# Attention steps inside the weight products: scores, transposes and output products put together behind twelve products

## The chip, the cores and the metric

One Trainium2 chip, one of its cores. The metric is the time of one execution on the device in microseconds (us); lower is better. TensorE is PE in the rows (its weight loads PEld), VectorE is DVE, ScalarE is ACT, GpSimd is POOL and SyncE, which issues most transfers, is SP.

## What is computed

Attention with two batches, 8 heads, 768 positions and a head size of 64; a query sees the first `n_global` positions and its own last `n_local`, with a bias by distance. Its output goes through two feed-forward layers.

```python
scores = scale * np.matmul(q, k.transpose(0, 1, 3, 2)) + bias
scores = np.where(keep, scores, -1000000000.0)
a = np.exp(scores - np.max(scores, axis=-1, keepdims=True))
a = a / (np.sum(a, axis=-1, keepdims=True) + 1e-09)
x = np.matmul(a, v)              # then 1536 tokens x 512
h = x @ w_in                     # 512 x 2048
x = (h * (1.0 / (1.0 + np.exp(-1.702 * h)))) @ w_out
h = np.maximum(x @ w2_in, 0.0)
out = h * h @ w2_out
```

## The kernel before

Attention is cut into 48 units: unit u is a tile of 128 queries and a pair of heads, so four units in a row make one tile of the attention's output. A unit has 256 keys, or 128 in the first tile of each batch. A unit passes through these helpers:

- `u_scores` (L243): two products on PE, one for each head, into two PSUM banks.
- `u_max` (L257): for each head one DVE operation that reads the scores from PSUM, adds the bias and takes the maximum, and a short read of the accumulator.
- `u_exp` (L280): on ACT.
- `u_norm`: on DVE a small addition (L271), a reciprocal (L273) and one multiply for each head (L318).
- `u_transpose` (L291, four on PE), `u_et` (L301, ACT copies them out of PSUM), `u_av` (L329, output products on PE).
- After the fourth unit of a tile: `x_hi` (L336, ACT) and `x_lo` (L341, DVE) split the output tile into two parts.

The first 19 units run in a stage of their own. The units from 19 on are woven into the first 16 steps of the feed-forward products. Step t has two half steps, each a call of `half(u, t, kind, block)`: the one of kind 0 holds the twelve products of `m_g1(t)` (L600) and that of kind 1 the twelve of `m_g2(t-1)` (L646); in step 0 the twelve of `m_g1(0)` are shared between both. In each half step the next weight slice is also prepared: `w_pre` (L464, ACT), `w_decode` in three DVE operations (L101, L105, L109), and `w_split`, whose upper part is copied by ACT (L486) and whose lower part is made on POOL (L487). In kind 0 the activation (`m_act`, L608, ACT) and `m_gate` (L626, DVE) follow the products; in kind 1 `m_split` splits the gated values on ACT (L616) and POOL (L617).

The schedule is manual: each engine runs its instructions in the order in which the code writes them, so that an instruction that waits holds up all behind it on its engine. Scores go to banks 5 and 6 (columns 0 to 255 of each), transposes to all of bank 5, outputs to bank 7. Bank 4 holds the products of `m_g1`. After the attention ends, at about 200 us of the span, the rest is feed-forward products that the change doesn't touch.

Of the kernel before, what the change touches and what calls it, by code (L numbers as in the profile page):

```python
# [8 lines left out]
F32 = mybir.dt.float32  # L9
# [105 lines left out]
def tile_kernel(ctx: ExitStack, tc: tile.TileContext, a: dict, out: bass.AP):  # L115
    nc = tc.nc
    ctx.enter_context(tc.manual_schedule())
    att = ctx.enter_context(tc.tile_pool(name="att", bufs=2))
    psum = ctx.enter_context(tc.tile_pool(name="psum", bufs=1, space=PSUM))
    banks = [psum.tile([128, 512], F32, name=f"bank{n}") for n in range(8)]  # L120
    turn = {}

    def ring(name, n, shape, dt=F32):
# [2 lines left out]
    def nxt(key, tiles):  # L126
        turn[key] = turn.get(key, -1) + 1
        return tiles[turn[key] % len(tiles)]
# [75 lines left out]
    nu = len(units)  # L204
    ur_t, uh_t, ul_t, sc_t, e_t, st_t, tr_t, et_t, xt_t = ({} for _ in range(9))

    start = [True]
# [13 lines left out]
    def bank(what):  # L221

        if start[0]:
            return nxt(what, {"av": banks[0:2], "sc": [banks[2:4], banks[4:6]], "tr": banks[6:8]}[what])

        return {"sc": banks[5:7], "tr": banks[5], "av": banks[7]}[what]

    def u_load(u):
        if u >= nu or u in ur_t:
# [6 lines left out]
    def u_scores(u):  # L236

        n = u_keys(u)[0]
        t = ur_t[u][0]
        ps = sc_t[u] = bank("sc")  # L240
        for e in range(2):
            h = slice(e * 64, e * 64 + 64)
            nc.tensor.matmul(  # L243
                ps[e][:, 0:n], lhsT=t[h, 0:128], rhs=t[h, 384 - n:384], start=True, stop=True
            )

    def u_keys(u):

        return (256, 0) if units[u][0] % QT else (128, 256)

    def u_max(u):
        p = units[u][1]
        ps = sc_t.pop(u)
        e_, st = e_r[u % 4], st_r[u % 4]
        n, d0 = u_keys(u)
        for e in range(2):
            nc.vector.tensor_tensor_reduce(  # L257
                out=e_[:, e, 0:n], in0=ps[e][:, 0:n], in1=dh[:, 2 * p + e, d0:d0 + n],
                scale=-0.125, scalar=3.0e38, op0=ALU.add, op1=ALU.min, accum_out=st[:, e:e + 1],
            )  # L260
        e_t[u], st_t[u] = e_, st
# [3 lines left out]
    def u_sum(u):  # L265

        if not 0 <= u < nu or sums.get(u) == 2:
            return
        st = st_t[u]
        if u not in sums:  # L270
            nc.vector.tensor_scalar_add(st[:, 4:6], st[:, 4:6], 1e-9)  # L271
        else:
            nc.vector.reciprocal(st[:, 6:8], st[:, 4:6])  # L273
        sums[u] = sums.get(u, 0) + 1

    def u_exp(u):
        e_, st = e_t[u], st_t[u]
        n = u_keys(u)[0]
        for e in range(2):
            nc.scalar.activation(  # L280
                out=e_[:, e, 0:n], in_=e_[:, e, 0:n], func=AF.Exp, scale=-1.0,
                bias=st[:, e:e + 1], accum_out=st[:, 4 + e:5 + e],
            )

    def u_transpose(u):
        e_ = e_t.pop(u)
        nb = u_keys(u)[0] // 128
        ps = bank("tr").rearrange("p (b q) -> p b q", b=2)
        for b in range(nb):
            for e in range(2):  # L290
                nc.tensor.transpose(  # L291
                    ps[:, b, e * 128:e * 128 + 128], e_[:, e, b * 128:b * 128 + 128], ident
                )
        tr_t[u] = ps

    def u_et(u, eng):
        ps = tr_t.pop(u)
        nb = u_keys(u)[0] // 128
        t = et_r[u % 2]
        if eng is nc.scalar:  # L300
            eng.copy(t[:, 0:nb], ps[:, 0:nb])  # L301
        else:
            eng.tensor_copy(t[:, 0:nb], ps[:, 0:nb])
        et_t[u] = t

    def u_norm(u, eng):
        u_sum(u)
        u_sum(u)
        e_, st = e_t[u], st_t.pop(u)
        n = u_keys(u)[0]  # L310
        if eng is nc.gpsimd:
            eng.tensor_tensor(
                out=e_[:, :, 0:n], in0=e_[:, :, 0:n],
                in1=st[:, 6:8].unsqueeze(2).to_broadcast([128, 2, n]), op=ALU.mult,
            )
        else:
            for e in range(2):
                eng.tensor_scalar_mul(e_[:, e, 0:n], e_[:, e, 0:n], st[:, 6 + e:7 + e])  # L318
# [19 lines left out]
    def x_lo(qt):  # L338
        c, i = divmod(qt, CH // 128)
        s = slice(i * 128, i * 128 + 128)  # L340
        nc.vector.tensor_tensor(  # L341
            out=xl[c][:, :, s], in0=xt_t.pop(qt), in1=xh[c][:, :, s].bitcast(F32), op=ALU.subtract
        )
# [29 lines left out]
    def u_out(u):  # L373
        if not 0 <= u < nu:
            return
        u_av(u)
        if units[u][1] == NP - 1:
            x_hi(units[u][0])
            los.append(units[u][0])

    def rest(inner):
# [41 lines left out]
        def plain(t):  # L423
            return steps[t][1] == 0
# [34 lines left out]
        def w_pre(kind, t):  # L459
            if (kind, t) not in raws or raws[kind, t][0] is None:  # L460
                return
            r, _ = raws[kind, t]
            c = mo.tile([128, 512], F32, tag=f"c{kind}", name=f"c{kind}", bufs=CB[kind])
            nc.scalar.activation(out=c, in_=r[:, :, 1].bitcast(F32), func=AF.Copy, scale=2.0 ** -112)  # L464
            raws[kind, t] = (r, c)

        def w_decode(kind, t, parts=range(3)):
            if (kind, t) not in raws or raws[kind, t][0] is None:
                return
            r, c = raws[kind, t]  # L470
            decode(nc, r, c, c, parts)
            ph, _, f = steps[t]
            if 2 in parts and kind == 1:
                nc.sync.dma_start(out=store[ph * NF + f], in_=c)
# [6 lines left out]
        def w_split(kind, t):  # L481
            if (kind, t) not in raws:
                return
            hi, lo = w_slot(kind, t)
            c = raws.pop((kind, t))[1]
            nc.scalar.copy(hi, c)  # L486
            nc.gpsimd.tensor_tensor(out=lo, in0=c, in1=hi.bitcast(F32), op=ALU.subtract)  # L487
            if kind == 1 or any(plan[t2][1] and uses[t2] == uses[t] for t2 in range(t + 1, T)):
                parts_out.append((kind, t, hi, lo))
# [99 lines left out]
        def h_bank(t):  # L589

            return banks[{0: 3, T0: 5, T0 + 1: 6}.get(t, 4)]
# [13 lines left out]
        def m_act(t):  # L605
            func, scale = ((AF.Tanh, 0.851), (AF.Relu, 1.0))[steps[t][0]]
            s = s_r[t % 2] if t >= T0 else sg[:, t % 3]
            nc.scalar.activation(out=s, in_=h_bank(t), func=func, scale=scale)  # L608
            g_t[t] = s

        def halves(x, n):

            return x[:, 1:3] if n else x[:, 0:8:7]
# [5 lines left out]
        def m_gate(t):  # L619
            s, h = g_t[t], h_bank(t)  # L620
            g = s
            if not plain(t):
                g = halves(g_p, t % 2)
                s, h = (x.rearrange("p (n k) -> p n k", n=2) for x in (s, h))
            if steps[t][0] == 0:
                nc.vector.scalar_tensor_tensor(out=g, in0=s, scalar=1.0, in1=h, op0=ALU.add, op1=ALU.mult)  # L626
            else:
                nc.vector.tensor_tensor(out=g, in0=h, in1=s, op=ALU.mult)  # L628


        def m_split(t):
            g = g_t[t]
            if t >= T0 and t % 2 == 0:
                ghl[t // 2 % 2] = mo.tile([128, 4, 512], F32R, tag="m4", name="ghl", bufs=2)
            gh, gl = (ghl[t // 2 % 2][:, t % 2 * 2 + n] for n in range(2))
            split(g, gh, gl, nc.vector if t >= T0 else nc.gpsimd)
            g_t[t] = (gh, gl)
# [273 lines left out]
        def half(u, t, kind, block):  # L911

            tw = t + 2 - kind
            w_pre(kind, tw)
            w_split(kind, tw - 1)
            block(0)
            if u < nu:
                u_scores(u)
            w_decode(kind, tw, (0,))
            w_decode(kind, tw, (1,))  # L920
            if u < nu:
                u_max(u)
                u_exp(u)
            block(1)
            if u <= nu:
                u_norm(u - 1, nc.vector)
            w_decode(kind, tw, (2,))
            if kind == (t == 0):
                m_act(t)
                m_gate(t)  # L930
            if kind == 1:
                m_split(t)
            if u - 2 < nu:
                u_transpose(u - 2)
                u_et(u - 2, nc.scalar)
            u_out(u - 3)
            if los:
                x_lo(los.pop())
            u_load(u + 4)

        u = n0 + 3
# [26 lines left out]
        for t in range(T0, T + LAG):  # L968
            q, e = divmod(t, 2)
# [306 lines left out]
```

## Time and profile before

| what | value |
|---|---|
| median of 3 runs (lowest, highest) | 647.03 us (645.46, 647.56) |
| the profiled execution's own time | 645.78 us |
| its span in the trace | 643.9 us |
| granted clock of TensorE, mean | 0.986 |
| PE busy | 617.9 us, 96% of the span |
| DVE busy | 480.6 us, 75% |
| ACT busy | 323.3 us, 50% |
| POOL busy | 93.1 us, 14% |

The span is what the trace covers; 1.9 us lie around it. Shares of busy time are means over stages that differ: the half steps lie between about 46 and 200 us.

### The profile page before, as it was taken

The numbers are of one execution on the slowest core, as the hardware profiler recorded it, in microseconds if no ns is written. First come the engines' busy times: TensorE is split into PE (matmuls) and PEld (weight loads), VectorE is DVE, ScalarE is ACT, GpSimd is POOL, SyncE is SP. The second block draws the span as 40 slices with busy tenths as digits, with TensorE's granted clock in tenths as the row PEclk, the third lists the DMA queues.
The fourth block names the chain that finished last, engine by engine and source line by source line (L and its number), as shares of the span: only waits on it lengthen the run. The fifth ranks groups of instructions, "written<-read, shape, count | busy, mean of one in ns | idle before, by whom it ended". The sixth has DMA issues, their size and how long they took to land.

```text
span 643.9 us, 10391 instructions
## 1 busy us (share of the span) xinstructions
PE 617.9 (96%) x3614; PEld 502.6 (78%) x3614; DVE 480.6 (75%) x1039; ACT 323.3 (50%) x632; POOL 93.1 (14%) x76
## 2 busy tenths in 40 slices
PE   7898999999999899999999999999999999999995
PEld 4555665666677798889999988788889999999995
DVE  5888998888773988686887788988577777656454
ACT  5785666677663544345444356555344344422332
POOL 3434544644541000000000000000000000000000
PEclk7989999999999999999999999999999999999998
DMA  7868698999836899980899978999579994058772
GB/s 216 280 190 265 220 312 286 314 309 302 292 134 231 277 342 357 379 310 1 266 378 379 403 271 290 350 303 353 192 249 343 331 315 168 17 196 304 270 259 72
DMA packets 74221, 172.69 MB, mean 268 GB/s; under 512 B 7728, under 2 KB 32432, under 8 KB 71088
## 3 DMA queue, kind: packets, MB, share of 16 engines
q1 hardware_dynamic: 63696, 139.69, 64.2%
q10 hardware_dynamic: 10464, 32.25, 12.5%
q8 instruction: 31, 0.51, 0.3%
q14 instruction: 30, 0.25, 0.1%
HBM read 117.64 MB, written 54.26 MB: 267 GB/s over the span
## 4 chain that ended last, share of the span: by engine, by line
PE 70%; DVE 13%; DMA 9%; ACT 3%; issue 2%; SPq 2%; DVEq 0%; ACTq 0%
PE bank L600 32%; PE bank L779 19%; PE bank L646 10%; DMA room<-store 4%; PE bank L329 3%; PE bank L243 3%; PE bank L291 3%; DVE c L105 3%; DMA raw<-in_wi_dram 2%; DMA wi<-store_in 2%; DVE room L677 2%; DVE c L101 1%; DVE room L257 1%; DVE c L109 1%; ACT room L301 1%
## 5 line engine op out<-in xcount | busy, mean ns | idle before, releaser
L600 PE MATMUL bank<-xh,wi 128*128 128x512 f32 x608 | 193.2, 398 | 4.8 <-DVE room L626 2.9
L600 PEld LDWEIGHTS bank<-xh,wi 128*128 128x128 f32 x608 | 108.8, 188 | 31.7 <-issue 5.4
L600 PE MATMUL bank<-xl,wi 128*128 128x512 f32 x304 | 119.0, 391 | 0.0
L608 ACT ACTIVATE room<-bank 128x512 f32<-128x512 f32 x80 | 47.7, 596 | 93.3 <-PE bank L600 92.7
L737 ACT CAST gf<-room 128x768 fp32r<-128x768 f32 (+1 forms) x62 | 58.5, 943 | 46.5 <-DVE room L677 21.4
L677 DVE TENSOR_TENSOR room<-room 128x256 f32<-128x256 f32 x192 | 73.0, 421 | 6.2 <-DMA room<-store 4.0
L628 DVE TENSOR_TENSOR room<-bank,room 128x512 f32<-128x512 f32 x48 | 33.2, 691 | 59.4 <-ACT room L608 59.4
L745 DVE TENSOR_TENSOR gf<-room,gf 128x768 fp32r<-128x768 f32 (+1 forms) x62 | 67.4, 1088 | 5.7 <-ACT gf L737 5.7
L280 ACT ACTIVATE room<-room,st 128x256 f32<-128x256 f32 (+1 forms) x96 | 46.3, 484 | 49.6 <-DVE st L257 49.6
L600 PEld LDWEIGHTS bank<-xl,wi 128*128 128x128 f32 x304 | 57.1, 188 | 13.2 <-DVE xl L341 0.4
L826 POOL TENSOR_TENSOR tmp<-tmp,tmp 128x512 f32<-128x512 f32 x1 | 1.3, 1297 | 435.6 <-DVE tmp L826 435.6
L646 PE MATMUL bank<-ghl,room_w 128*128 128x512 f32 x192 | 52.4, 409 | 0.0
L600 PE MATMUL bank<-xh,q 128*128 128x512 f32 x160 | 50.9, 399 | 0.0
L105 DVE SCALAR_TENSOR_TENSOR c<-raw,c 128x512 int32<-128x512 int32 x64 | 47.5, 742 | 2.1
L109 DVE SCALAR_TENSOR_TENSOR c<-raw,c 128x512 int32<-128x512 int32 x64 | 45.9, 717 | 1.1
L779 PEld LDWEIGHTS bank<-gf,room_r 128*128 128x128 f32 x336 | 42.3, 191 | 3.4 <-ACT room L608 2.2
L779 PE MATMUL bank<-gf,room_r 128*128 128x256 f32 x336 | 42.8, 283 | 1.8 <-ACT room L608 1.8
L646 PEld LDWEIGHTS bank<-ghl,room_w 128*128 128x128 f32 x192 | 33.9, 188 | 12.5 <-issue 6.2
L779 PEld LDWEIGHTS bank<-gf,room_w 128*128 128x128 f32 x336 | 42.4, 191 | 1.2
L779 PEld LDWEIGHTS bank<-room_r,gf 128*128 128x128 f32 x336 | 42.4, 191 | 1.2
L779 PEld LDWEIGHTS bank<-room_w,gf 128*128 128x128 f32 x336 | 42.2, 191 | 1.1
L779 PE MATMUL bank<-room_r,gf 128*128 128x256 f32 x336 | 42.8, 283 | 0.0
(98 smaller groups left out, 944.4 us busy)
## 6 DMA issues: line engine op xcount, KB each, us to landing
wi<-store_in SPq DMA_DIRECT2D x76, 256.0 KB, 5.8
raw<-in_wi_dram SPq DMA_DIRECT2D x32, 512.0 KB, 5.6
raw<-in_wo_dram SPq DMA_DIRECT2D x32, 512.0 KB, 5.6
room_w<-store_p SPq DMA_DIRECT2D x6, 1792.0 KB, 7.8
room_r<-store_p SPq DMA_DIRECT2D x6, 1792.0 KB, 8.4
room<-in_units_dram SPq DMA_DIRECT2D x48, 192.0 KB, 4.0
room<-store SPq DMA_DIRECT2D x32, 256.0 KB, 6.3
room<-in_units_dram SPq DMA_DIRECT2D x48, 128.0 KB, 3.9
```

The lines of the kernel that those rows point to most:

```text
L105: nc.vector.scalar_tensor_tensor(out=o, in0=hi, scalar=-0x80000000, in1=o, op0=ALU.bitwise_and, op1=ALU.bitwise_or)
L109: nc.vector.scalar_tensor_tensor(out=o, in0=lo, scalar=29, in1=o, op0=ALU.logical_shift_right, op1=ALU.bitwise_or)
L243: nc.tensor.matmul(ps[e][:, 0:n], lhsT=t[h, 0:128], rhs=t[h, 384 - n:384], start=True, stop=True)
L280: nc.scalar.activation(out=e_[:, e, 0:n], in_=e_[:, e, 0:n], func=AF.Exp, scale=-1.0, bias=st[:, e:e + 1], accum_out=st[:, 4 + e:5 + e],)
L600: nc.tensor.matmul(h_bank(t), lhsT=l[:, w], rhs=r[c][:, kt, :], start=(k == 0), stop=(k == 3 * KT - 1))
L608: nc.scalar.activation(out=s, in_=h_bank(t), func=func, scale=scale)
L628: nc.vector.tensor_tensor(out=g, in0=h, in1=s, op=ALU.mult)
L646: nc.tensor.matmul(o, lhsT=l[:, b], rhs=r, start=(t in (0, T1) and n3 == 0), stop=(t in (T0 - 1, T1 + T0 - 1) and n3 == 2),)
L677: nc.vector.tensor_tensor(out=x[:, dst], in0=x[:, l], in1=x[:, r], op=getattr(ALU, op))
L737: nc.scalar.copy(d[:, :, 0], g_p[:, s])
L745: nc.vector.tensor_tensor(out=d[:, :, 1], in0=g_p[:, s], in1=d[:, :, 0].bitcast(F32), op=ALU.subtract)
L779: nc.tensor.matmul(banks[BANK[n]][:, b * 256:b * 256 + 256], lhsT=l[:, b * 128:b * 128 + 128], rhs=r, start=(first and b == 0 and n3 == 0) ...
```

## The change

Three things change, all for the half steps. The twelve products of a half step stand together, and scores, transposes and output products follow them. On DVE, the order in a half step becomes: norm of unit u-2, maximum of unit u-1, the three decodes, the gate; the exponentials of unit u-1 go with the maximum. And the transposes no longer go to bank 5 but to the upper halves (columns 256 to 511) of the two banks whose lower halves hold the scores; the two banks become one tile, `banks`, for that.

```diff
-    banks = [psum.tile([128, 512], F32, name=f"bank{n}") for n in range(8)]
+    banks = [psum.tile([128, 512], F32, name=f"bank{n}") for n in range(6)]
+    two = psum.tile([128, 2, 512], F32, name="banks")
+    banks[5:5] = [two[:, 0], two[:, 1]]
...
-        return {"sc": banks[5:7], "tr": banks[5], "av": banks[7]}[what]
+        return {"sc": banks[5:7], "tr": two[:, :, 256:512], "av": banks[7]}[what]
...
             block(0)
-            if u < nu:
-                u_scores(u)
+            block(1)
+            if u - 2 in st_t:
+                u_norm(u - 2, nc.vector)
+            if u - 1 in sc_t:
+                u_max(u - 1)
+                u_exp(u - 1)
             w_decode(kind, tw, (0,))
             w_decode(kind, tw, (1,))
-            if u < nu:
-                u_max(u)
-                u_exp(u)
-            block(1)
-            if u <= nu:
-                u_norm(u - 1, nc.vector)
             w_decode(kind, tw, (2,))
             if kind == (t == 0):
                 m_act(t)
                 m_gate(t)
+            if u < nu:
+                u_scores(u)
             if kind == 1:
                 m_split(t)
```

In the rows below, line numbers of the changed kernel are 2 to 4 higher (L245 is L243 of before, L295 is L291, L333 is L329). PE in a half step of kind 0, before: two blocks of six products (L600), with the two scores (L243) between them.

```order
L600 MATMUL bank_67<-xh_71,wi_218 128x512 x2
L600 MATMUL bank_67<-xl_72,wi_218 128x512
L600 MATMUL bank_67<-xh_71,wi_218 128x512 x2
L600 MATMUL bank_67<-xl_72,wi_218 128x512
L243 MATMUL bank_68<-room 128x128
L243 MATMUL bank_69<-room 128x128
L600 MATMUL bank_67<-xh_71,wi_218 128x512 x2
L600 MATMUL bank_67<-xl_72,wi_218 128x512
L600 MATMUL bank_67<-xh_71,wi_218 128x512 x2
L600 MATMUL bank_67<-xl_72,wi_218 128x512
L291 MATMUL bank_68<-ident,room 128x128 x4
L329 MATMUL bank_70<-room 64x128 x4
```

The same on PE in the changed kernel:

```order
L604 MATMUL bank_67<-xh_70,wi_217 128x512 x2
L604 MATMUL bank_67<-xl_71,wi_217 128x512
L604 MATMUL bank_67<-xh_70,wi_217 128x512 x2
L604 MATMUL bank_67<-xl_71,wi_217 128x512
L604 MATMUL bank_67<-xh_70,wi_217 128x512 x2
L604 MATMUL bank_67<-xl_71,wi_217 128x512
L604 MATMUL bank_67<-xh_70,wi_217 128x512 x2
L604 MATMUL bank_67<-xl_71,wi_217 128x512
L245 MATMUL banks<-room 128x128 x2
L295 MATMUL banks<-ident,room 128x128 x4
L333 MATMUL bank_68<-room 64x128 x4
```

The scores have moved from the middle of the products to their end; nothing else has moved on PE.

DVE in the first half steps in which an output tile ends (kind 1, `x_lo`) and the half step after it, before: the split of the output (L341), two decodes, the maximum (L257), then the norm (L271, L273, L318).

```order
L341 TENSOR_TENSOR xl_209<-bank_70,xh_208 128x4x128
L101 TENSOR_SCALAR c_749<-c_749 128x512
L105 SCALAR_TENSOR_TENSOR c_749<-raw_650,c_749 128x512
L257 ISA room,st_86<-bank_68,dh 128x256
L257 ISA st_86 128x1
L257 ISA room,st_86<-bank_69,dh 128x256
L257 ISA st_86 128x1
L271 TENSOR_SCALAR st_85<-st_85 128x2
L273 RECIPROCAL st_85<-st_85 128x2
L318 TENSOR_SCALAR room<-room,st_85 128x256 x2
L109 SCALAR_TENSOR_TENSOR c_749<-raw_650,c_749 128x512
L626 SCALAR_TENSOR_TENSOR sg<-sg,bank_67 128x512
```

The same on DVE in the changed kernel (L345 is the split of the output):

```order
L345 TENSOR_TENSOR xl_208<-bank_68,xh_207 128x4x128
L273 TENSOR_SCALAR st_83<-st_83 128x2
L275 RECIPROCAL st_83<-st_83 128x2
L322 TENSOR_SCALAR room<-room,st_83 128x256 x2
L259 ISA room,st_84<-banks,dh 128x256
L259 ISA st_84 128x1
L259 ISA room,st_84<-banks,dh 128x256
L259 ISA st_84 128x1
L101 TENSOR_SCALAR c_740<-c_740 128x512
L105 SCALAR_TENSOR_TENSOR c_740<-raw_641,c_740 128x512
L109 SCALAR_TENSOR_TENSOR c_740<-raw_641,c_740 128x512
L630 SCALAR_TENSOR_TENSOR sg<-sg,bank_67 128x512
```

Norm and maximum now follow directly on the split, and the three decodes stand in a row behind them; the scores of the half step, at the end of its products, wait for that maximum, which reads the banks they write. The order on POOL and on SP is unchanged.

## Rows read from the trace of the kernel before

**Rows 1.** The page: busy time of each engine, share of the span, instructions.
```profile
PE 617.9 (96%) x3614; PEld 502.6 (78%) x3614; DVE 480.6 (75%) x1039; ACT 323.3 (50%) x632; POOL 93.1 (14%) x76
```

**Rows 2.** Windows: stretch, its length, busy us and instructions by engine, clock, DMA.
```profile
60.00:70.00 10.00, 9.74 (x56) 6.55 (x56) 9.24 (x25) 6.77 (x17) 4.78 (x3) 1.00 0.70 219
80.00:90.00 10.00, 9.27 (x54) 6.33 (x54) 9.54 (x26) 6.29 (x17) 4.32 (x3) 1.00 0.87 295
...
150.00:160.00 10.00, 10.00 (x59) 6.88 (x58) 7.81 (x24) 6.82 (x18) 4.80 (x3) 1.00 0.94 301
```

**Rows 3.** Timeline of PE, one half step: start, us, engine, line, operation, [idle before].
```profile
139.95 1.67 PE L646 MATMUL bank<-ghl,room_w 128*128 128x512 f32 x6
141.55 0.70 PE L243 MATMUL bank<-room 64*128 64x256 f32 x4
142.19 1.66 PE L646 MATMUL bank<-ghl,room_w 128*128 128x512 f32 x6
143.69 0.60 PE L291 MATMUL bank<-ident,room 128*128 128x128 f32 x4
144.22 0.66 PE L329 MATMUL bank<-room 128*64 128x128 f32 x8
144.81 0.50 PE L600 MATMUL bank<-xh,wi 128*128 128x512 f32 x1
```

**Rows 4.** Timeline of PE, the first half step without scores.
```profile
188.45 3.06 PE L646 MATMUL bank<-ghl,room_w 128*128 128x512 f32 x12
191.35 0.60 PE L291 MATMUL bank<-ident,room 128*128 128x128 f32 x4
```

**Rows 5.** Waits of PE: the sum (us, times, longest), then timeline of PE.
```profile
PE bank L291 <- DVE st L257: 3.5, 6, 1.0
...
56.93 0.70 PE L243 MATMUL bank<-room 64*128 64x256 f32 x4 [1.17 <-ACT room L301]
...
78.19 0.73 PE L600 MATMUL bank<-xh,wi 128*128 128x512 f32 x2
...
80.33 0.66 PE L291 MATMUL bank<-ident,room 128*128 128x128 f32 x4 [0.48 <-DVE st L257]
80.92 0.66 PE L329 MATMUL bank<-room 128*64 128x128 f32 x8
```

**Rows 6.** Timeline of DVE and POOL where both want SBUF.
```profile
68.15 1.29 POOL L487 TENSOR_TENSOR wi<-c,wi 128x512 fp32r<-128x512 f32 x1 [0.31 <-DVE c L101]
68.16 1.82 DVE L105 SCALAR_TENSOR_TENSOR c<-raw,c 128x512 int32<-128x512 int32 x1
...
75.57 1.74 DVE L318 TENSOR_SCALAR room<-room,st 128x256 f32<-128x256 f32 x2
75.87 1.30 POOL L617 TENSOR_TENSOR ghl<-sg,ghl 128x512 fp32r<-128x512 f32 x1 [0.56 <-ACT ghl L616]
...
112.88 0.69 DVE L105 SCALAR_TENSOR_TENSOR c<-raw,c 128x512 int32<-128x512 int32 x1
112.93 1.79 POOL L487 TENSOR_TENSOR room_w<-c,room_w 128x512 fp32r<-128x512 f32 x1 [2.50 <-DVE c L101]
```

**Rows 7.** Timeline of DVE: one maximum and one norm, with no hindrance.
```profile
69.91 0.41 DVE L257 CUSTOM_DVE_ANT_0 room<-bank,dh 128x256 f32<-128x256 f32 x1
...
70.59 0.16 DVE L271 TENSOR_SCALAR st<-st 128x2 f32<-128x2 f32 x1
...
70.99 0.62 DVE L318 TENSOR_SCALAR room<-room,st 128x256 f32<-128x256 f32 x2
```

**Rows 8.** Timeline of all engines where an output tile has just ended.
```profile
125.41 0.73 PE L600 MATMUL bank<-xh,wi 128*128 128x512 f32 x2
...
126.14 0.69 DVE L341 TENSOR_TENSOR xl<-bank,xh 128x512 fp32r<-128x512 f32 x1 [0.85 <-ACT xh L336]
...
126.75 0.42 DVE L101 TENSOR_SCALAR c<-c 128x512 int32<-128x512 int32 x1
...
127.27 1.78 POOL L487 TENSOR_TENSOR wi<-c,wi 128x512 fp32r<-128x512 f32 x1 [0.83 <-ACT wi L486]
```

More of the change, by code (lines that the diff above doesn't have):

```diff
@@ L287, in u_transpose @@
         nb = u_keys(u)[0] // 128
-        ps = bank("tr").rearrange("p (b q) -> p b q", b=2)
+        ps = bank("tr")
+        if start[0]:
+            ps = ps.rearrange("p (b q) -> p b q", b=2)
         for b in range(nb):
```

## The prediction, made before the changed kernel was run

> **What bounds the kernel now.** I read the page first: PE is busy for 96% of the span and DVE for 75% [rows 1], so PE sets the end over the whole. The change touches the half steps alone, so the next view is the windows. At 150 to 160 us PE shows no idle time and DVE works 7.81 of 10 us; at 60 to 70 and 80 to 90 PE has 0.26 and 0.73 us of idle time and DVE works 9.24 and 9.54 us [rows 2]. So there are two regimes: early on PE waits for a DVE that is nearly full, later PE runs through. TensorE's granted clock is 1.00 in all three windows, its upper level of 2.4 GHz, and I count nothing for it.
>
> The timeline of PE gives the undisturbed half step [rows 3]. From first product to first product: products to scores 1.60 us, scores to products 0.64, products to transposes 1.50, transposes to output products 0.53, these to the next products 0.59; together 4.86 us. The waits name what PE waits for early on: the transposes, for the maximum on DVE, since both use bank 5. That is 3.5 us in six waits, and one wait of the scores for the copy of the transposes adds 1.17 us [rows 5].
>
> **PE's own time.** Twelve products in a row take 2.90 us up to the transposes [rows 4]; before scores it is 0.10 us more, as 1.60 stands to 1.50 [rows 3], so 3.00. No row shows transposes right behind scores. The nearest is products behind scores, 0.64; I take it, with 0.53 (the step from transposes to output products) and 0.74 us (0.64 and the 0.10 of the other seam) as ends. Transposes that start after a pause take 0.59 to the output products (80.33 to 80.92) [rows 5], and the return to the products stays 0.59. The new half step is 3.00 + 0.64 + 0.59 + 0.59 = 4.82 us, a gain of 0.04. Units 19 to 47 give 29 half steps: 29 x 0.04 = **1.2 us gained** (ends: 29 x 0.15 = 4.4 gained, 29 x 0.06 = 1.7 lost). So little, because the scores leave one seam and make another: scores, then another kind of product.
>
> The Trainium skill says, in "TensorEngine Tiling (Array Packing)", Key Properties, that changing the tiling mode drains the engine. Scores use half the rows and output products half the columns, so by that rule there are four changes of mode in a half step before and four after, and the gain would be 0 in place of 1.2; the rows agree with a price at each seam, but show 0.64 against 0.53 and not one equal price.
>
> **The waits that go.** The transposes get other columns than the scores and come after them, so the maximum of the same unit no longer stands ahead of them; the early scores come later than the copy they waited for. The seven waits are 3.5 + 1.17 = 4.7 us of idle time. A wait costs more than its gap: from 78.19 to 80.33 are 2.14 us in place of 1.50, 0.64 for a gap of 0.48 [rows 5]. With 0.16 for each of seven: **5.8 us gained** at most. That a new wait comes in their place is the next term.
>
> **What is late next: the scores, for the maximum.** Scores of a half step now wait until both maxima of the unit before have left banks 5 and 6, and on DVE norm (of the unit before that) and maximum stand first in the half step. In most half steps DVE reaches them early: the decodes are behind, and the scores are due only 3.00 us after the first product. But in every fourth half step the output tile ends, and DVE's split of it (L341) stands ahead. It can't move forward: it waits for ACT's copy, which waits for the last output product. I place the new order on the times of such a half step, counted from its first product at 125.41 [rows 8]:
>
> - The split runs at 0.73 to 1.42; the next DVE operation starts at 1.34 (126.75).
> - The norm begins there instead of the decode. Its multiplies start 0.40 after it (70.59 to 70.99), and two take 0.62, so each about 0.35 with an overlap [rows 7]. The first runs at 1.74 to 2.09.
> - POOL's operation of this half step (L487) comes at 1.86 (127.27), in the middle of that multiply. It hangs on ACT's copies, which keep their places.
>
> DVE and POOL hold each other up when both work in SBUF. Where POOL came first, by 0.01 us, L105 took 1.82 in place of 0.69, 1.13 more; where it came during the first of the two multiplies (75.87), the pair took 1.74 in place of 0.62, 1.12 more, so the waiting POOL operation goes ahead of the second multiply; where it came 0.05 after L105's start it waited itself, 1.79 in place of 1.30 [rows 6]. Here the second case holds. POOL starts at 2.09 and runs some 1.16 us (from 113.57, L105's end, to 114.72), the second multiply ends 0.14 after it as at 77.31 [rows 6], at 3.39; the maximum starts at 3.31 and takes 0.68 and a short accumulator read of 0.08 [rows 7], so it is done at 4.07. The scores were due at 3.00: **PE waits 1.07 us, some 1.1 with the signal**. Without POOL the maximum would be done at 3.03, and PE would wait 0.03 to 0.07.
>
> Such half steps with scores follow those of u = 22, 26 ... 46: seven. 7 x 1.1 = **7.7 us lost** (ends 0.5 and 7.7).
>
> "SBUF — State Buffer" in the Trainium skill, Who interferes with whom, speaks against this change too: the port pair that DVE and GpSimd share is an exclusive lock, and who starts first holds it for the whole instruction. By it the price would be a whole POOL operation of 1.30 us, 7 x 1.30 = 9.1 in place of 7.7; the trace has 1.12 to 1.13.
>
> **What follows on such a wait.** After it DVE is later in its queue by about as much, and POOL has two more operations in each pair of half steps that can fall into norm or decodes, now that three decodes stand in a row and the maximum, which did run beside POOL, no longer stands between them. Whether another 1.1 us comes due at the scores of one of the next half steps is a matter of some 0.1 us in arrival, which I can't settle from this trace. Between none and one for each of seven, 0 to 7.7, I take half: **3.9 us lost**.
>
> **Costed at nothing.** The exponentials go with the maximum, half a step later; their readers, the norms, stand a half step behind them, and ACT has idle time (6.82 of 10 us busy [rows 2]). Unit loads on SP wait for the scores, now 1.4 us later in the half step (3.00 in place of 1.60); SP's other transfers stand behind that, but a unit is loaded four half steps ahead, some 19 us. If that cover were gone, 1.4 us would be paid once or twice. The gate waits for the same twelve products as before.
>
> **The sum**, against the profiled execution's 645.78: 645.78 - 1.2 - 5.8 + 7.7 + 3.9 = 650.4 us. The median of the runs shown, 647.03, lies 1.25 above that execution, so I expect 651.6 and say 651.5.
>
> **The rivals.**
>
> *Faster: DVE stays ahead of PE.* If POOL's operation arrives after the first multiply has ended (2.09 in place of 1.86, by a later weight slice or ACT copy), the second multiply is not held up, and the seven waits shrink to 0.07. Then 645.78 - 1.2 - 5.8 + 0.5 = 639.3, at the median's level 640.5. It decides at 0.23 us. For it: DVE works only 7.81 of 10 us later on [rows 2]. Against it: the split can't come earlier.
>
> *Balanced: the seven waits come, and nothing follows.* 645.78 - 1.2 - 5.8 + 7.7 = 646.5, at the median's level 647.7: no change that can be told.
>
> *DVE becomes the bound.* Per pair of half steps DVE works 0.78 x 9.7 = 7.6 us, and three POOL operations could add 3 x 1.1 = 3.3: 10.9 against PE's 9.64. If 2.5 of 3 hit on the mean, a pair takes 10.35, 0.7 above; 14 pairs, 10 us, stand in place of 7.7 + 3.9 and less. With all three, 17 us: 645.78 - 7.0 + 17.6 = 656.4, at the median's level 657.6.
>
> *The change does not do what it says:* the engines' order shows that it does, so this gets no chance.
>
> **How the numbers follow.** The forecast has 0.50, faster 0.23, balanced 0.22, DVE as the bound 0.05. About 0.3%, 1.9 us, is what a measurement of this kernel can tell from no change: faster is below 645.1, slower above 649.0. That gives faster 0.23, same 0.22, slower 0.55. The range must reach into the faster case and up to the full bound on DVE: 641 to 658; outside it lies the end of the faster case and a few in a hundred above. The forecast's own range is 647.7 to 656.
>
> **What would show it.** Right: in the changed trace PE's scores show waits for DVE's maximum (L259) of about 1.1 us in the half steps after an output tile ended, the second norm multiply there takes 1.4 us beside POOL's L491, no transposes wait for a maximum, and an undisturbed half step takes 4.8 us. Wrong: scores that never wait, half steps of 4.8 us throughout and DVE with idle time ahead of its decodes; or a half step whose undisturbed length is well off 4.82, by the unseen seam from scores to transposes.

## The result, and the profile after

| what | before | after |
|---|---|---|
| median of 6 runs each (lowest, highest) | 647.29 us (645.46, 648.52) | 652.90 us (650.55, 653.54) |
| ratio of the runs, 95% interval | | 1.0089 [1.0069, 1.0108] |
| the profiled execution's own time | 645.78 us | 653.23 us |
| its span in the trace | 643.9 us | 651.4 us |
| granted clock of TensorE, mean | 0.986 | 0.980 |

The changed kernel is slower by 0.9%. The page of after has one line on the engines, to be held against [rows 1]:

```profile
PE 618.6 (95%) x3614; PEld 505.2 (78%) x3614; DVE 501.0 (77%) x1039; ACT 325.3 (50%) x632; POOL 85.1 (13%) x76
```

PE's own work has not changed. DVE shows 20.4 us more with the same 1039 instructions, POOL 8.0 us less with the same 76. An instruction that is held up counts as busy, so where DVE and POOL meet, it is now DVE that is held.

The windows of after (stretch, its length, then busy us and instructions of PE, PEld, DVE, ACT, POOL, granted clock, DMA share, GB/s), the last three those of [rows 2]:

```profile
0.00:50.00 50.00, 42.54 (x265) 24.99 (x265) 34.27 (x151) 34.83 (x110) 18.76 (x28) 0.80 0.69 209
...
60.00:70.00 10.00, 8.72 (x53) 6.21 (x54) 8.87 (x20) 6.87 (x18) 4.38 (x4) 1.00 0.79 258
80.00:90.00 10.00, 9.79 (x59) 7.08 (x58) 9.72 (x24) 6.45 (x17) 4.43 (x4) 1.00 0.88 296
150.00:160.00 10.00, 8.89 (x55) 6.06 (x54) 9.72 (x24) 6.30 (x17) 4.01 (x3) 1.00 0.92 304
```

At 60 to 70 us PE idles for 1.28 us where it idled for 0.26, at 80 to 90 us for 0.21 in place of 0.73. At 150 to 160 us PE had run through, with DVE at 7.81 of 10 us [rows 2]; now PE idles for 1.11 us and DVE shows 9.72.

**Where the time is.** I take the stage of the half steps from its first product to the end of its last output products. In the timeline of PE, before and then after (start, us, engine, line, operation):

```profile
46.61 0.74 PE L600 MATMUL bank<-xh,wi 128*128 128x512 f32 x2 [0.21 <-ACT xh L336]
...
199.44 0.66 PE L329 MATMUL bank<-room 128*64 128x128 f32 x8
```

```profile
49.07 0.73 PE L604 MATMUL bank<-xh,wi 128*128 128x512 f32 x2 [0.22 <-ACT xh L340]
...
206.53 0.66 PE L333 MATMUL bank<-room 128*64 128x128 f32 x8
```

That is 200.10 - 46.61 = 153.5 us before and 207.19 - 49.07 = 158.1 after, 4.6 more. The two spans differ by 7.5: 4.6 in this stage, 2.5 ahead of it (49.07 against 46.61) and 0.4 behind it. The code of what lies ahead is untouched, but the change reaches it all the same: of the two banks that are now one tile, `banks`, the first stage uses one for scores and the other for transposes. The maximum there (L259) now waits for ACT's copy of transposes (L305) six times, 6.6 us in all, and before it waited for no such copy. That this makes the later start is not shown: the first experiment has the same tile and 5.4 us of such waits, and its stage starts at 46.61 us, as before. Over nine traces the stage began between 46.6 and 50.3 us, in the latest case in a kernel that is faster than both. So the stage's length is the yardstick for the experiments, beside the times, and what makes the 2.5 us stays open.

**The half step now.** Timeline of PE in after, an undisturbed half step and the one that follows the end of an output tile, as [rows 3] and [rows 8] of before:

```profile
123.78 3.04 PE L650 MATMUL bank<-ghl,room_w 128*128 128x512 f32 x12
126.75 0.70 PE L245 MATMUL banks<-room 64*128 64x256 f32 x4
127.38 0.66 PE L295 MATMUL banks<-ident,room 128*128 128x128 f32 x4
127.97 0.66 PE L333 MATMUL bank<-room 128*64 128x128 f32 x8
128.56 0.74 PE L604 MATMUL bank<-xh,wi 128*128 128x512 f32 x2
...
132.73 0.70 PE L245 MATMUL banks<-room 64*128 64x256 f32 x4 [1.11 <-issue]
```

From 123.78 to 128.56 are 4.78 us, against 4.86 in [rows 3]; products to scores 2.97, then 0.63, 0.59 and 0.59. In the second one the scores come 4.17 us after the first product (128.56 to 132.73). "issue" means that the profile shows no releaser for the 1.11 us; by the program the scores write the banks that DVE's maximum (L259) still reads. DVE and POOL at the same place:

```profile
129.29 0.69 DVE L345 TENSOR_TENSOR xl<-bank,xh 128x512 fp32r<-128x512 f32 x1 [0.16 <-ACT xh L340]
129.90 0.16 DVE L273 TENSOR_SCALAR st<-st 128x2 f32<-128x2 f32 x1
...
130.30 1.65 DVE L322 TENSOR_SCALAR room<-room,st 128x256 f32<-128x256 f32 x2
...
131.87 0.41 DVE L259 CUSTOM_DVE_ANT_0 room<-banks,dh 128x256 f32<-128x256 f32 x1
...
132.21 0.41 DVE L259 CUSTOM_DVE_ANT_0 room<-banks,dh 128x256 f32<-128x256 f32 x1
```

```profile
130.41 1.39 POOL L491 TENSOR_TENSOR wi<-c,wi 128x512 fp32r<-128x512 f32 x1 [1.82 <-ACT wi L490]
```

POOL's L491 arrives 0.11 us after the pair of norm multiplies has begun; the pair takes 1.65 us in place of the 0.62 of [rows 7], ends at 131.95, just behind POOL's 131.80, and the second maximum ends at 132.62. The scores start 0.11 later.

There are seven such half steps, as the prediction counted. Their step from products to scores takes 4.18, 3.95, 4.34, 4.17, 4.17, 4.18 and 4.25 us: over 3.00 that is 8.2 us in all. Seven more half steps, between 51 and 112 us, have scores that come late, by 4.2 us together, counted in the same way; the longest of them (1.28 us at 66.07) is this, in the timelines of POOL, DVE and PE:

```profile
63.12 1.29 POOL L491 TENSOR_TENSOR room_w<-c,room_w 128x512 fp32r<-128x512 f32 x1 [1.75 <-ACT room_w L490]
```

```profile
63.15 1.28 DVE L273 TENSOR_SCALAR st<-st 128x2 f32<-128x2 f32 x1
```

POOL was ahead by 0.03 us, and an addition on 128 x 2 numbers, 0.16 us by itself, took 1.28 and held norm and maximum behind it. No transposes wait for a maximum any more.

### The profile page after: what moved, and what is told of

Read it like the earlier page. It is cut to its first block, busy times and chain, and to the rows that moved or that the text cites. A ratio compares the mean times of both kernels' runs of the same rounds, so it can differ in the third digit from the quotient of the medians.

```text
span 651.4 us, 10389 instructions
## 1 busy us (share of the span) xinstructions
PE 618.6 (95%) x3614; PEld 505.2 (78%) x3614; DVE 501.0 (77%) x1039; ACT 325.3 (50%) x632; POOL 85.1 (13%) x76
## 4 chain that ended last, share of the span: by engine, by line
PE 77%; DVE 8%; DMA 7%; issue 3%; SPq 2%; ACT 1%; ACTq 0%; DVEq 0%
PE bank L604 35%; PE bank L783 14%; PE bank L650 9%; PE banks L783 6%; PE bank L333 3%; PE banks L295 3%; PE banks L650 3%; PE banks L245 3%; DMA store_p<-room_w 2%; DMA wi<-store_in 2%; DMA room<-store 1%; PE bank L245 1%; DVE c L105 1%; DMA room_w<-store_p 1%; DVE c L109 1%
## 5 line engine op out<-in xcount | busy, mean ns | idle before, releaser
L604 PE MATMUL bank<-xh,wi 128*128 128x512 f32 x600 | 189.3, 396 | 3.6 <-DVE room L630 1.9
L109 DVE SCALAR_TENSOR_TENSOR c<-raw,c 128x512 int32<-128x512 int32 x64 | 56.4, 882 | 2.1
L650 PE MATMUL bank<-ghl,room_w 128*128 128x512 f32 x192 | 48.5, 400 | 0.0
L604 PE MATMUL bank<-xh,q 128*128 128x512 f32 x152 | 47.8, 396 | 0.0
L105 DVE SCALAR_TENSOR_TENSOR c<-raw,c 128x512 int32<-128x512 int32 x64 | 45.2, 707 | 2.1
L245 PE MATMUL banks<-room 64*128 64x256 f32 (+1 forms) x134 | 27.2, 425 | 11.7 <-issue 11.1
L101 DVE TENSOR_SCALAR c<-c 128x512 int32<-128x512 int32 x64 | 36.5, 571 | 0.2 <-ACT c L468 0.2
L333 PE MATMUL bank<-room 128*64 128x128 f32 x352 | 31.9, 301 | 3.2 <-DVE room L307 2.1
L630 DVE SCALAR_TENSOR_TENSOR room<-room,bank 128x512 f32<-128x512 f32 x30 | 20.6, 685 | 16.3 <-ACT room L612 16.2
L333 PEld LDWEIGHTS bank<-room 128*64 128x64 f32 x352 | 19.4, 144 | 16.8 <-ACT room L305 5.6
L604 PEld LDWEIGHTS bank<-xh,q 128*128 128x128 f32 x152 | 27.5, 188 | 6.1 <-issue 0.7
```

Of the source, the lines that this page charges most:

```text
L105: nc.vector.scalar_tensor_tensor(out=o, in0=hi, scalar=-0x80000000, in1=o, op0=ALU.bitwise_and, op1=ALU.bitwise_or)
L109: nc.vector.scalar_tensor_tensor(out=o, in0=lo, scalar=29, in1=o, op0=ALU.logical_shift_right, op1=ALU.bitwise_or)
L245: nc.tensor.matmul(ps[e][:, 0:n], lhsT=t[h, 0:128], rhs=t[h, 384 - n:384], start=True, stop=True)
L333: nc.tensor.matmul(xt_t[qt][e * 64:e * 64 + 64, p], lhsT=v[:, b * 128 + e * 64:b * 128 + e * 64 + 64], rhs=t[:, b, e * 128:e * 128 + 128], ...
L604: nc.tensor.matmul(h_bank(t), lhsT=l[:, w], rhs=r[c][:, kt, :], start=(k == 0), stop=(k == 3 * KT - 1))
L650: nc.tensor.matmul(o, lhsT=l[:, b], rhs=r, start=(t in (0, T1) and n3 == 0), stop=(t in (T0 - 1, T1 + T0 - 1) and n3 == 2),)
```

## The experiments

My theory (A where the expectations use letters) is that the scores wait because DVE and POOL lock each other out in the row of split, norm and maximum. Its rival is that this row is too long by itself, whatever POOL does. Two more questions go with it: do the other columns give anything by themselves, or do the guards between the engines (the semaphores that the program sets) go by bank (D); and can the waits be removed for good, or do they only move? Ratios are against runs of the kernel before on the same chip.

**The split of the output behind the maximum.** The kernel after; x_lo stands behind the exponentials of the next half step, and once behind the last step:

```diff
                 u_exp(u - 1)
+            if los:
+                x_lo(los.pop())
             w_decode(kind, tw, (0,))
...
             u_out(u - 3)
-            if los:
-                x_lo(los.pop())
...
+        x_lo(los.pop())
```

> The changed kernel, but the split of an ended output tile (x_lo, L345) stands behind the maximum of the next half step in place of ahead of its norm. Theory A (the split holds back norm and maximum, and POOL's operation then falls into the norm's first multiply): the seven waits of the scores of 1.1 to 1.2 us, 8.2 us together with their refill, go, and the time falls from 652.9 to about 645 (643.5 to 647). Theory B (DVE is late in these half steps anyway, by its whole load in a pair of half steps): the waits shrink by less than half, to 649 to 652.

Measured: 647.45 us (12 runs) against 645.98 (23 runs), ratio 1.0017 [0.9998, 1.0036]. The time is above the range that the theory gave, 643.5 to 647, though before was 1.3 us faster here than in the result's runs. The stage takes 152.2 us, 5.9 less than after. PE and then DVE:

```profile
102.51 0.70 PE L245 MATMUL banks<-room 64*128 64x256 f32 x4 [1.31 <-issue]
...
118.36 0.70 PE L245 MATMUL banks<-room 64*128 64x256 f32 x4 [0.74 <-issue]
...
123.11 0.70 PE L245 MATMUL banks<-room 64*128 64x256 f32 x4
```

```profile
144.97 0.62 DVE L322 TENSOR_SCALAR room<-room,st 128x256 f32<-128x256 f32 x2
145.50 0.42 DVE L259 CUSTOM_DVE_ANT_0 room<-banks,dh 128x256 f32<-128x256 f32 x1
...
146.18 0.69 DVE L345 TENSOR_TENSOR xl<-bank,xh 128x512 fp32r<-128x512 f32 x1
```

The row at 123.11 comes 4.75 us after the one ahead of it, and from there no scores wait. So the place of x_lo is a needed part of the loss after an ended tile. This alone doesn't part the lock from its rival, since taking x_lo away shortens the row and also moves the norm off POOL's operation. Up to 119 us eight waits of the scores remain, 6.0 us.

**POOL's operation later, after an ended tile alone.** The kernel after:

```diff
-            w_split(kind, tw - 1)
+            if not (u % 4 == 3):
+                w_split(kind, tw - 1)
...
                 u_exp(u - 1)
+            if u % 4 == 3:
+                w_split(kind, tw - 1)
```

> The changed kernel with the split of the output where it is; only in the half step after an ended tile (u % 4 == 3) ACT's copy and POOL's operation of the weight split stand behind the maximum and the exponentials, so that POOL can't come during the norm. If the lock between DVE and POOL is the price (theory A), the second multiply of the norm takes 0.35 us there in place of 1.38, the scores wait 0.05 to 0.15 in place of 1.1, and the time falls by 7 x 1.0 = 7 us to about 646 (644.5 to 648). If the position of the split alone is the price (theory C), the waits of 1.1 stay and the time stays at 652 to 653.

Measured: 653.65 us (6 runs), ratio 1.0122 [1.0092, 1.0153]; stage 159.2 us. DVE with POOL, then PE:

```profile
127.60 0.69 DVE L345 TENSOR_TENSOR xl<-bank,xh 128x512 fp32r<-128x512 f32 x1 [0.16 <-ACT xh L340]
...
128.61 0.62 DVE L322 TENSOR_SCALAR room<-room,st 128x256 f32<-128x256 f32 x2
...
133.11 1.71 DVE L322 TENSOR_SCALAR room<-room,st 128x256 f32<-128x256 f32 x2
```

```profile
133.38 1.29 POOL L491 TENSOR_TENSOR room_w<-c,room_w 128x512 fp32r<-128x512 f32 x1 [0.53 <-ACT room_w L490]
```

```profile
130.01 0.70 PE L245 MATMUL banks<-room 64*128 64x256 f32 x4
...
135.60 0.70 PE L245 MATMUL banks<-room 64*128 64x256 f32 x4 [0.77 <-issue]
```

In the half step after the ended tile the multiplies take 0.62 and the scores come 3.14 us after the first product (126.87 by the timeline): the row of split, norm and maximum is short enough by itself, and the rival falls. But the expected 646 did not come; the time alone would have spoken for the other theory. POOL, late once, falls into the norm of the next half step (1.71) and of the one after (1.72 at 138.71), and the scores wait 0.77 and 0.74 there. The price is handed on.

**The other columns alone.** The kernel before, with nothing but the transposes in the upper halves of the two banks, and the tile `banks` that this needs:

```diff
-        return {"sc": banks[5:7], "tr": banks[5], "av": banks[7]}[what]
+        return {"sc": banks[5:7], "tr": two[:, :, 256:512], "av": banks[7]}[what]
```

> The kernel before with only the change of banks: transposes go to the upper halves of the two banks that hold the scores, the order on all engines as before. Theory D (the guard between the engines goes by bank, not by column): the transposes still wait, now for both maxima in place of the first one; where PE waited already, seven times early on, 0.35 us more each: 647.3 + 2.4 = 649.7 at most, 647 to 650. Theory E (other columns free the transposes of the wait for the maximum, as the prediction counted it): the waits of 3.5 us and their refill go, 642 to 644.

Measured: 646.26 us (median of 13 runs, one of them 3277.81), ratio 1.0002 [0.9982, 1.0023]. Other columns of the same banks give nothing measurable, as theory D expects; theory E had 642 to 644. The kept trace is of the execution of 3277.81 us, with PE busy for 100% of the span, so no wait of PE can be compared in it. The trace of after has rows on the guard: ACT's copy of transposes (L305) and the maximum that waits for it, first in the first stage, then in a half step:

```profile
20.04 0.59 ACT L305 COPY room<-banks 128x512 f32<-128x512 f32 x1 [0.51 <-PE banks L295]
20.66 0.42 DVE L259 CUSTOM_DVE_ANT_0 room<-banks,dh 128x256 f32<-128x256 f32 x1 [1.81 <-ACT room L305]
...
59.09 0.42 DVE L259 CUSTOM_DVE_ANT_0 room<-banks,dh 128x256 f32<-128x256 f32 x1 [0.35 <-ACT room L305]
```

The Trainium skill asks for such a guard in "PSUM — Partial Sum Buffer", PSUM bank collisions raise a hardware error: semaphores should guard PSUM by bank (and quadrant of partitions), not by address. The row at 59.09 agrees: maximum and copy use other columns of the same banks, and the maximum waits. The row at 20.66 is a wider guard than that: there the maximum reads one bank and the copy the other, and they share only the tile. So the wait may go by the tile that joins the two banks as well as by the bank; no run has the other columns without the joined tile.

**POOL late in the order of before.** The kernel before, with the waits of the transposes for the maximum as the target:

```diff
-            w_split(kind, tw - 1)
             block(0)
...
                 u_exp(u)
+            w_split(kind, tw - 1)
             block(1)
```

> The kernel before; in every half step ACT's copy and POOL's operation of the weight split stand behind the maximum and the exponentials. Before, the early waits of the transposes came where POOL's operation stood 0.01 to 0.5 us ahead of a decode that precedes the maximum. If the lock is their cause (theory A), the early waits for the maximum go, 4 to 6 us: 641.5 to 644. If DVE's plain load is their cause (theory B), or if POOL's operation now only hits the norm and the third decode and the delay is handed on, 646 to 648.

Measured: 651.12 us (6 runs), ratio 1.0079 [1.0051, 1.0107]; stage 158.1 us, as long as in after, by another way. POOL, DVE, PE:

```profile
116.97 1.29 POOL L487 TENSOR_TENSOR room_w<-c,room_w 128x512 fp32r<-128x512 f32 x1 [3.43 <-DMA raw<-in_wo_dram]
118.21 1.28 POOL L617 TENSOR_TENSOR ghl<-sg,ghl 128x512 fp32r<-128x512 f32 x1
```

```profile
118.44 1.33 DVE L101 TENSOR_SCALAR c<-c 128x512 int32<-128x512 int32 x1 [1.37 <-ACT c L464]
```

```profile
120.90 0.66 PE L291 MATMUL bank<-ident,room 128*128 128x128 f32 x4 [0.44 <-DVE st L257]
...
131.26 0.66 PE L291 MATMUL bank<-ident,room 128*128 128x128 f32 x4 [0.45 <-DVE st L257]
```

Two POOL operations now stand in a row, the second (L617) holds the first decode (1.33 where [rows 8] show 0.42), the maximum behind it is late, and in every second half step the transposes wait 0.44. Again the same lock, at another place. Both expectations were missed, and what makes the early waits of before is not shown by this run.

**The maximum first.** The kernel after:

```diff
-            if u - 2 in st_t:
-                u_norm(u - 2, nc.vector)
             if u - 1 in sc_t:
                 u_max(u - 1)
                 u_exp(u - 1)
+            if u - 2 in st_t:
+                u_norm(u - 2, nc.vector)
```

> The changed kernel with one exchange on DVE: the maximum of unit u-1 stands ahead of the norm of unit u-2. The scores then wait for nothing but the maximum, and a POOL operation that falls into the norm holds back the transposes alone, which are due 0.6 us later. Theory A (the seven waits of 1.2 us are norm plus lock standing ahead of the maximum): in the seven half steps after an ended tile the scores wait no more, and the transposes wait about 0.5 us for the norm in place of 1.2; the other early waits of the scores (4.2 us) go too or shrink to a third. 652.9 - 8.2 + 3.5 - 3 = 645 (643.5 to 647). Theory B (DVE is short of time over a pair of half steps): the waits only move to the transposes with their whole size, 650 to 653.

**The maximum first, then the norm, then the split.** The same, with x_lo behind both; its old place goes as in the first experiment:

```diff
+            if u - 2 in st_t:
+                u_norm(u - 2, nc.vector)
+            if los:
+                x_lo(los.pop())
             w_decode(kind, tw, (0,))
...
```

> As the run with the maximum ahead of the norm, and in addition the split of an ended output tile stands behind both. Theory A: no wait of scores or transposes after the first few half steps, each half step 4.81 us; against the run with the split moved alone, whose trace still had waits of 6.2 us in the early half steps, 3 to 6 us less: 641.5 to 645 where the kernel before stands at 646 to 647. Theory B: the early waits stay, since DVE with the locks is full there (9 of 10 us): 646 to 648.

Measured against 646.85 (23 runs of before): 648.85 us (12 runs), ratio 1.0031 [1.0009, 1.0053], and 648.64 (12 runs), 1.0019 [0.9997, 1.0041]; stages 154.7 and 153.9 us. Both missed the range of the theory: the first lies between those of its two theories, the second just above that of its rival. POOL and DVE of the first of them, then PE:

```profile
156.96 1.28 POOL L491 TENSOR_TENSOR wi<-c,wi 128x512 fp32r<-128x512 f32 x1 [2.27 <-ACT wi L490]
```

```profile
157.02 1.24 DVE L273 TENSOR_SCALAR st<-st 128x2 f32<-128x2 f32 x1
158.29 0.17 DVE L275 RECIPROCAL st<-st 128x2 f32<-128x2 f32 x1
158.50 0.62 DVE L322 TENSOR_SCALAR room<-room,st 128x256 f32<-128x256 f32 x2
```

```profile
157.75 0.70 PE L245 MATMUL banks<-room 64*128 64x256 f32 x4
158.91 0.81 PE L295 MATMUL banks<-ident,room 128*128 128x128 f32 x4 [0.46 <-DVE room L322]
```

After ended tiles the scores wait no more, but for 0.16 us once. But the norm, now behind the maximum, is held by POOL (1.24 for L273), and the transposes of the same half step need that norm: 0.46 us here, 0.25 in the second kernel (at 138.58). In both, from 114 us on, every second half step takes 4.9 to 5.5 us in place of 4.8. A wait for the maximum has become a wait for the norm.

**Without POOL.** The kernel after; in the half steps POOL's subtraction for the lower part of the weights is left out, and ACT copies the weight slice there:

```diff
-            nc.gpsimd.tensor_tensor(out=lo, in0=c, in1=hi.bitcast(F32), op=ALU.subtract)
+            (nc.scalar.copy(lo, c) if not start[0] else nc.gpsimd.tensor_tensor(out=lo, in0=c, in1=hi.bitcast(F32), op=ALU.subtract))
```

> The changed kernel with POOL's subtraction of the weight split (L491) left out in the half steps: ACT copies the weight slice there in its place, so the lower parts hold other numbers; POOL keeps the subtraction of the gated values (L621), and nothing else changes. If the lock between DVE and POOL is what makes the scores wait (theory A), the seven waits of 1.2 us shrink to 0.1 and most of the early ones go: 652.9 - 7.5 - 3 = 642.5 (640.5 to 645). If the split of the output and DVE's own load make them (theory C), less than half of the waits goes: 649 to 653.

Measured against 645.47 (17 runs of before): 640.3 us (6 runs), ratio 0.9915 [0.9885, 0.9945]; stage 146.4 us. The time is 0.2 us below the range of theory A, with before 1.8 us faster here than in the result's runs. PE after an ended tile:

```profile
143.81 0.63 PE L604 MATMUL bank<-xh,wi 128*128 128x512 f32 x2
144.27 0.40 PE L604 MATMUL bank<-xl,wi 128*128 128x512 f32 x1
144.75 0.70 PE L245 MATMUL banks<-room 64*128 64x256 f32 x4
```

The order of DVE is that of after, x_lo ahead of norm and maximum, and still the gap ahead of these scores is 0.07 us, 3.15 from the first product (141.60). Early on 0.25 and 0.07 are left. With POOL's operation gone the waits are gone: they need both DVE's order and POOL's operation in it. That ACT has one more copy in each half step does not undo this. It also shows what this operation of POOL costs the stage: without it the stage is 11.7 us shorter than in after.

**The norm a half step ahead, between the decodes.** The kernel after, x_lo behind the maximum, and the norm of the unit whose maximum has just been taken between the second and third decode, so that the transposes that need it come a half step later:

```diff
-            if u - 2 in st_t:
-                u_norm(u - 2, nc.vector)
             if u - 1 in sc_t:
                 u_max(u - 1)
                 u_exp(u - 1)
+            if los:
+                x_lo(los.pop())
             w_decode(kind, tw, (0,))
             w_decode(kind, tw, (1,))
+            for v in (u - 2, u - 1):
+                if v in st_t:
+                    u_norm(v, nc.vector)
             w_decode(kind, tw, (2,))
...
```

> As the run with the split of an ended output tile behind the maximum, but the maximum is the first of a half step on DVE, and the norm of the same unit stands between the second and the third decode, as in the kernel before: a whole half step ahead of its transposes. Theory A: scores wait only where DVE is late by more than 2 us, the transposes never; the early waits of 6.2 us fall to 1 to 3 and the later half steps stay at 4.8 us: 641.5 to 645 where the kernel before stands at 646 to 647. Theory B (the sum of DVE's work and of the locks decides early on, not its order): as with the split moved alone, 645 to 648.

Measured against the same 645.47: 642.15 us (12 runs), ratio 0.9952 [0.9933, 0.9971], faster than both kernels and as theory A expected; stage 148.6 us. POOL, DVE, PE:

```profile
140.03 1.29 POOL L621 TENSOR_TENSOR ghl<-sg,ghl 128x512 fp32r<-128x512 f32 x1 [1.36 <-DVE st L275]
```

```profile
140.04 1.69 DVE L322 TENSOR_SCALAR room<-room,st 128x256 f32<-128x256 f32 x2
```

```profile
136.00 3.02 PE L650 MATMUL bank<-ghl,room_w 128*128 128x512 f32 x12
138.94 0.70 PE L245 MATMUL banks<-room 64*128 64x256 f32 x4
139.57 0.66 PE L295 MATMUL banks<-ident,room 128*128 128x128 f32 x4
140.16 0.66 PE L333 MATMUL bank<-room 128*64 128x128 f32 x8
140.75 0.74 PE L604 MATMUL bank<-xh,wi 128*128 128x512 f32 x2
```

The norm is still held, 1.69 in place of 0.62, and nobody waits: 4.75 us from 136.00 to 140.75. So the lock is still there, but its price can be put where there is time. Its stage still has waits of scores of 1.23, 0.36 and 1.01 us, the last at 100.84.

## Why the prediction was right

It said 651.5 us, slower, with a range of 641 to 658; the median is 652.90.

- **What bounds the kernel, and the two regimes:** right. Granted clock 1.00 in all three windows, PE running through later, waiting for DVE earlier.
- **PE's own time,** 4.82 us for a half step and 1.2 us gained: slightly low. The undisturbed half steps take 4.75 to 4.81, mean over the two kinds 4.79 against 4.85 of before, 29 x 0.06 = 1.7 us gained (an estimate). The seam that no row showed, from scores to transposes, is 0.63 where I took 0.64.
- **The waits that go,** 5.8 us: right in kind; no transposes wait for a maximum, in any window. The size was not measured apart. Of its two reasons, other columns and a later place, the first did not hold: the run with the other columns alone gains nothing (1.0002).
- **The scores after an ended tile,** 7.7 us: right in place, in mechanism and nearly in size. Worked out: POOL at 1.86 us from the first product, the pair of multiplies done at 3.39, the maximum at 4.07, a wait of 1.1. Measured at 128.56: 1.85, 3.39, 4.06 and 1.11. Seven such half steps, 8.2 us over 3.00. That POOL makes it is shown by the run without it (0.07 us of wait with DVE's order unchanged); that x_lo's place is the other half, by the run that moves it.
- **What follows on such a wait,** 3.9 us: right in size by 4.2, in place only in part. I expected it behind the ended tiles. Four of the seven late scores, 2.3 us, do come one to three half steps behind such a wait (81.71, 96.27, 101.44 and 106.49); the other three come ahead of the first, and after 112 us none follows. All lie in the early regime, where DVE is nearly full. In five the trace has a norm held by POOL (63.15, 79.49, 94.21, 97.88, 104.05) and in one a decode ahead of the norm (51.31); in the seventh the maximum waited 0.35 us for ACT's copy (59.09 above). The figure was the middle between two ends and its nearness is luck.
- **The sum:** -1.7 - 5.8 + 8.2 + 4.2 = +4.9 by the measured terms, with 5.8 taken from the prediction, against +4.6 in the stage; the prediction had +4.6.
- **The level:** I added 1.25 us for the median over the profiled execution; the medians differ by 5.6, of which the stage explains 4.6. The other 1.0 us lies within what the intervals leave open (1.0069 to 1.0108 is 4.5 to 7.0 us).
- **The faster rival** had the right point of decision: 0.23 us in POOL's arrival. After's POOL came at 1.85 in place of 2.09. But the runs show more than the rival said: let POOL come later, and the next half steps pay (1.0122). DVE as the bound, the third rival, did not come: from 112 us on only the half steps after an ended tile are long, every other one keeps to PE's 4.8 us.

The lock was first taken at 1.12 us from the rows of before. The rows after have 1.65 - 0.62 = 1.03 and 1.28 - 0.16 = 1.12, in both less than POOL's whole operation beside it, 1.39 and 1.29. Of the 1.39 some 0.1 is POOL's own wait for the first multiply, an estimate from the 1.27 to 1.30 that its operations take in this trace where they come first. "SBUF — State Buffer" in the Trainium skill, Who interferes with whom, has the one that starts first hold the shared ports for its whole instruction; the kind of it agrees, the amount is 0.17 (1.12 against 1.29) and 0.36 us lower here (1.03 against 1.39, where POOL began 0.11 us into the pair).

**What stays open.** The first experiment starts its stage at the same 46.61 us as before and ends it 1.3 us sooner (152.2 to 153.5), yet its time is that of before or slightly above. Behind the stage its trace has 644.2 - 198.84 = 445.4 us and before's 643.9 - 200.10 = 443.8. PE doesn't give the gain back: its last product ends 436.5 us behind the stage there and 436.7 in before. The difference lies behind that last product, 8.9 us to the end of the span against 7.1, where results are added and stored; over the nine traces this end takes 6.9 to 8.9 us. Whether it depends on the change, one trace of each kernel can't tell. And differences under about 0.3%, such as between the two kernels with the maximum first, can't be told by these runs.

## What to carry to other kernels

Where two engines lock each other out, a new order of one engine is judged by where the other's operations fall in it, on a time line of one period: adding up start times from rows of the old trace gave that wait to within 0.1 us in the four late half steps here. Moving the operation that holds the lock handed its price to the next work (1.0079 in the order of before, 1.0122 in that of after); what helped was to put work that someone waits for soon, here the maximum, ahead of it, and to let the lock fall on work that was done a half step early. Check after such a move what the next engine in the chain needs: with the maximum first the norm became late, and of the kernels that leave nothing out only the one with the norm a half step ahead beat the kernel before. And a tile that joins two banks can bring waits where neither the code nor its order has changed, as it did in the first stage.

## What the runs showed of the hardware that was not expected

- A small DVE operation pays as much as a large one: an addition on 128 x 2 numbers took 1.28 us in place of 0.16 beside a POOL operation that began 0.03 us ahead of it (63.12 and 63.15), and 1.24 at 157.02 in the run with the maximum first.
- A POOL operation that arrives within a DVE operation goes ahead of the DVE operation queued behind it, though that one stands ready: 130.41 within the first of two multiplies, and the pair ends at 131.95, 0.15 us behind POOL. The same shows at 133.38 and in [rows 6].
